# Head sums of a sliding-window attention by four accumulating DMAs, on one Trainium2 core

## The chip, the cores and the metric

The kernel runs on one core of a Trainium2 chip. The metric is the device time of one execution in microseconds (us). Before the change it is 1233.46 us (median of 3 runs, 1233.28 to 1234.1). A ratio of two kernels is the mean time of one kernel's runs over that of the other's of the same rounds, so it is not quite the ratio of the medians that are quoted.

Engines: PE is TensorE's matmul, PEld its weight load, DVE is VectorE, ACT is ScalarE, POOL is GpSimd, SP is SyncE.

## The reference

Two identical layers of attention and a dense GELU block, in bfloat16, over 2048 tokens of width 1024. Attention has 32 heads of 32 dimensions. Each token sees 8 keys: its own and those 2, 4, ..., 14 tokens back.

```python
def _A_ref(x, wqkv, wo):
    B, S, D = x.shape
    H = 32; Dh = D // H
    W, dil = 8, 2
    qkv = (x @ wqkv).reshape(B, S, 3, H, Dh).transpose(2, 0, 3, 1, 4)
    q, k, v = qkv[0], qkv[1], qkv[2]
    idx = jnp.arange(S)[:, None] - (jnp.arange(W) * dil)[None, :]
    mask = idx >= 0
    ...                                     # kg, vg: k and v at idx
    logits = jnp.einsum("bhsd,bhswd->bhsw", q, kg) * Dh ** -0.5
    logits = jnp.where(mask[None, None, :, :], logits, -1e9)
    o = jnp.einsum("bhsw,bhswd->bhsd", _softmax(logits, axis=-1), vg)
    return o.transpose(0, 2, 1, 3).reshape(B, S, D) @ wo

def _B_ref(x, w1, b1, w2, b2):              # F = 3584
    return _gelu(x @ w1 + b1) @ w2 + b2

x = x + _A_ref(_layernorm(x), wqkv, wo);  x = x + _B_ref(_layernorm(x), w1, b1, w2, b2)   # twice
```

## The kernel before

The work is cut into 8 groups: 2 layers of 4 token groups of 512 tokens each. Groups 0 to 3 are the first layer. A group of 512 tokens is four token tiles of 128 (`NTT = 4`). TensorE does the projections of all groups one after the other. VectorE computes the attention of one group while TensorE is busy with another.

The head dimension lies as follows. Head h's 32 dimensions are spread over 8 chunks c and over four partitions 4h + j. VectorE multiplies q and the eight shifted k's of a chunk into `prod[128, 4 tiles, 8 shifts, 128 tokens]` (the tile is called `big` in the profile, and there are only three such buffers), and adds the eight chunks together. What remains is the *head sum*: adding the four partitions j of each head. The kernel before had two ways to do this.

- For groups 0 and 1, TensorE multiplies by a matrix of ones and zeros, `smat`, 32 columns wide; the four token tiles go to four strips of partitions of one PSUM tile `L`.
- For groups 2 to 7, four DMAs copy the four token tiles into another large buffer `Lq`, and VectorE adds its four slices.

```python
def head_sum(n, last=True):                  # groups 0 and 1
    ...
    for wh in range(2):
        for tb in range(NTT):
            mm(L[tb * H:(tb + 1) * H, wh * 4:(wh + 1) * 4, :], lhsT=smat[:],
               rhs=prod[:, tb, wh * 4:(wh + 1) * 4, :], start=start,
               stop=last, skip_group_check=True, tile_position=(0, tb * H))

def gather(n):                               # groups 2 to 7
    s = st[n]
    prod = s["prods"].pop(0)
    Lq = bigp.tile([P, HP, W, P], BF16, name="big")
    for tb in range(NTT):
        pool.dma_start(Lq[tb * H:(tb + 1) * H, :, :, :], prod[:, tb, :, :])

def attend(n):
    e = smp.tile([P, W, P], F32, name="e")
    if "Lq" in s: ...                        # three adds of Lq's slices into e; L = e
    else:
        head_sum(n)
        L = s.pop("L")
    ...                                      # mask; mx = max over w; e = L - mx
    act.on = 1 < n < N - 1                   # exp in program order among ACT's other work
    act.activation(e[:], e[:], ACT.Exp, scale=SCALE)
    act.on = False
    ...                                      # z = 1 / sum over w; a = e * z

def spread(n):                               # weights to all partitions, by way of DRAM
    for tb in range(NTT):
        pool.dma_start(a_d[:, :, tb * P:(tb + 1) * P], a[tb * H:(tb + 1) * H, :, :])
    for j in range(HP):
        pool.dma_start(abc[j::HP, :, :], a_d[:, :, :])
```

`av(n, c)` then forms the weighted sums over v, chunk by chunk, into `oT` (8 chunks of about 4.3 us of VectorE), and `gen_wo(n)` multiplies `oT` by the output projection. `act.copy` and `act.activation` also empty TensorE's PSUM banks: q, k and v chunks are cast out, and the dense block's hidden values go through GELU into `hT`. PSUM is the memory, in banks, that TensorE's sums go to and that the other engines empty. TensorE fills one bank (8 matmuls of 512 columns) in 1.72 us: while it runs without a wait, ScalarE's casts start 1.72 to 1.73 us apart.

The schedule around the first two groups; `(u, f)` means that f is put in after step u of TensorE's generator, and `hold` pins VectorE's program order:

```python
stage(q1, sides=at(6, attend, 0) + at(6, spread, 0) + at(6, hold) + each(new_prod, 1, 8, 1, 0, 4) + each(av, 0, 12, 1))
q2 = gen_qkv(2, defer=True)
stage(q2, 18)
new_prod(1, 4)
...
stage(gen_wo(0))
...
stage(gen_ffn1(0), sides=at(5, attend, 1) + at(5, spread, 1) + at(5, hold) + each(new_prod, 2, 2, 1)
      + at(10, gather, 2) + at(10, hold) + each(av, 1, 10, 2, 0, 4))
...
for n in range(1, N - 2):
    ...
    gather(n + 2)
    stage(gen_ffn1(n), sides=(at(20, attend, n + 2) if n + 3 == N else []) + each(av, n + 1, 8, 2, 3, 8))
```

## Time and profile before

| | before |
|---|---|
| time, median | 1233.46 us |
| span of the profiled execution | 1231.1 us |
| TensorE busy | 1226.2 us |
| VectorE busy | 870.0 us |
| TensorE's waits that the profile lists | 1.1 and 0.7 us |

The page of the kernel before begins with busy time by engine. PEclk is the granted clock of TensorE, that is the share of its full speed at which the chip lets it run, in tenths in 40 equal slices of the span (9 is 90% or more). The last line is the chain of work that ended last, by engine.

```profile
span 1231.1 us, 13996 instructions
...
PE 1226.2 (100%) x5789; PEld 632.7 (51%) x5789; DVE 870.0 (71%) x892; ACT 307.1 (25%) x491; POOL 123.0 (10%) x230
...
PEclk9999999999999999999999999999999999999999
...
PE 99%; DVE 0%; DMA 0%; ACT 0%; issue 0%
```

The list of TensorE's waits before: what waited, for whom; total us, times, longest.

```profile
PE acc L118 <- DVE big L93: 1.1, 1, 1.1
PE L L213 <- ACT xnT L93: 0.7, 1, 0.7
```

Both waits lie in the start-up. So TensorE bounds the kernel and nothing else costs time now. But the margin is thin in two places. VectorE's timeline before, around the end of group 0's weighted sums (columns: start, busy us, instruction, count, and in brackets the idle time just before it with what ended it):

```profile
123.41 0.76 DVE L93 TENSOR_TENSOR oT<-big 128x512 bf16<-128x512 bf16 x2
124.08 2.29 DVE L93 TENSOR_TENSOR big<-qT,kT 128x4096 bf16<-128x4096 bf16 x1
...
247.00 0.76 DVE L93 TENSOR_TENSOR oT<-big 128x512 bf16<-128x512 bf16 x2
```

TensorE's timeline at the same places:

```profile
125.40 13.99 PE L118 MATMUL acc<-wt,oT 128*128 128x512 bf16 x64
...
246.94 13.98 PE L118 MATMUL acc<-wt,oT 128*128 128x512 bf16 x64
```

`oT` of group 0 is complete at 124.17, and TensorE starts on it at 125.40: 1.2 us to spare. `oT` of group 1 is complete at 247.76, after TensorE has started at 246.94; only because the last chunks are needed last does nothing wait.

### The profile page before, as it was taken

What the parts mean: (1) busy time and instruction counts of PE and PEld (TensorE: products, weight loads), DVE (VectorE), ACT (ScalarE), POOL (GpSimd) and SP (SyncE); (2) the same over time, 40 slices, a digit from 0 to 9 for tenths busy, and PEclk for the clock granted to TensorE, in tenths of its full rate; (3) what the DMA queues carried; (4) which work ended last, traced back from release to release, by engine and by line L of the source; (5) the groups of instructions that cost most, each with busy time, mean ns of one, the idle gap of its engine ahead of it and who ended that gap; (6) DMA issues with size and microseconds to landing.
All of it is one profiled execution on the core that took longest, in us unless ns stands there. A gap on an engine that the chain in (4) does not pass through costs nothing.

```text
span 1231.1 us, 13996 instructions
## 1 busy us (share of the span) xinstructions
PE 1226.2 (100%) x5789; PEld 632.7 (51%) x5789; DVE 870.0 (71%) x892; ACT 307.1 (25%) x491; POOL 123.0 (10%) x230
## 2 busy tenths in 40 slices
PE   9999999999999999999999999999999999999999
PEld 7666544456444564445544465444654444444444
DVE  8989899995996999376992779927599698012001
ACT  4343152014310143202431024310244101400310
POOL 3010011101021102200031000210000102000000
PEclk9999999999999999999999999999999999999999
DMA  9954677756487658756476565766666569546441
GB/s 301 289 179 142 177 220 183 210 140 230 147 197 226 177 165 180 220 170 186 149 187 222 172 171 169 174 222 196 171 183 157 186 200 198 166 158 196 153 136 53
DMA packets 219359, 226.63 MB, mean 184 GB/s; under 512 B 68562, under 2 KB 187488, under 8 KB 216224
## 3 DMA queue, kind: packets, MB, share of 16 engines
q1 hardware_dynamic: 214704, 208.69, 57.1%
q0 software_dynamic: 4592, 17.05, 5.7%
q8 instruction: 45, 0.74, 0.2%
q14 instruction: 18, 0.15, 0.0%
HBM read 197.40 MB, written 6.29 MB: 165 GB/s over the span
## 4 chain that ended last, share of the span: by engine, by line
PE 99%; DVE 0%; DMA 0%; ACT 0%; issue 0%
PE acc L118 99%; DMA x<-in_A_x_dram 0%; DVE stats L93 0%; PE acc L213 0%; PE L L118 0%; PE L L213 0%; ACT xnT L93 0%; DVE xn L93 0%; DVE x L93 0%; DVE mv L93 0%; PE acc L183 0%; DVE rstd L93 0%
## 5 line engine op out<-in xcount | busy, mean ns | idle before, releaser
L118 PE MATMUL acc<-xnT,wt 128*128 128x512 bf16 (+1 forms) x3392 | 720.8, 375 | 0.0
L118 PEld LDWEIGHTS <-wt 128*128 128x128 bf16 x3392 | 400.3, 119 | 318.8 <-issue 1.6
L118 PE MATMUL acc<-wt,hT 128*128 128x512 bf16 (+1 forms) x1820 | 388.1, 376 | 0.0
L118 PEld LDWEIGHTS <-hT 128*128 128x128 bf16 x1820 | 178.1, 98 | 209.0
L93 DVE TENSOR_TENSOR big<-big 128x2048 bf16<-128x2048 bf16 (+2 forms) x184 | 245.6, 1360 | 2.9
L93 ACT ACTIVATE hT<-acc,b1T 128x512 bf16<-128x512 f32 x224 | 152.5, 688 | 331.3 <-PE acc L118 331.2
L93 DVE TENSOR_TENSOR big<-qT,kT 128x4096 bf16<-128x4096 bf16 x64 | 143.8, 2286 | 26.7 <-ACT kT L93 26.1
L93 DVE TENSOR_TENSOR big<-abc,vT 128x4096 bf16<-128x4096 bf16 x64 | 144.8, 2287 | 24.3 <-DMA abc<-a_d 23.7
L93 DVE TENSOR_TENSOR tmp<-acc,b2bc 128x512 f32<-128x512 f32 x56 | 38.7, 690 | 148.4 <-PE acc L118 144.9
L93 ACT CAST qT<-acc 128x512 bf16<-128x512 f32 (+1 forms) x72 | 38.0, 542 | 341.4 <-PE acc L118 341.4
L118 PE MATMUL acc<-wt,oT 128*128 128x512 bf16 x448 | 97.9, 379 | 0.0
L93 DVE BATCH_NORM_STATS2 stats<-x 128x6 f32<-128x512 bf16 x128 | 83.5, 680 | 3.3 <-DMA x<-in_A_x_dram 2.6
L118 PEld LDWEIGHTS <-oT 128*128 128x128 bf16 x448 | 43.9, 98 | 52.8
L93 DVE TENSOR_TENSOR x<-acc,big 128x512 bf16<-128x512 f32 (+1 forms) x9 | 5.7, 633 | 90.0 <-PE acc L118 90.0
L93 POOL TENSOR_TENSOR rstd<-mv,eps_t 128x1 f32<-128x1 f32 x56 | 22.5, 402 | 434.4 <-DVE mv L93 434.3
L93 ACT CAST vT<-acc 128x512 bf16<-128x512 f32 x64 | 37.5, 586 | 83.1 <-PE acc L118 83.1
L93 ACT CAST kT<-acc 128x512 bf16<-128x512 f32 x64 | 37.3, 588 | 66.7 <-PE acc L118 66.6
L93 DVE TENSOR_TENSOR x<-acc,x 128x512 bf16<-128x512 f32 x64 | 42.6, 669 | 3.9 <-PE acc L118 3.8
L93 POOL TENSOR_TENSOR rstd<-rstd,mhalf 128x1 f32<-128x1 f32 x56 | 41.6, 743 | 4.4
L93 DVE TENSOR_SCALAR xn<-x,mv,rstd 128x1024 bf16<-128x1024 bf16 x52 | 28.4, 546 | 17.1 <-POOL rstd L93 16.9
L93 DVE TENSOR_TENSOR x<-tmp,x 128x512 bf16<-128x512 f32 x56 | 38.6, 690 | 1.6
L93 DVE TENSOR_REDUCE z<-e 128x128 f32<-128x1024 f32 x8 | 15.4, 1926 | 33.7 <-ACT e L93 33.7
(64 smaller groups left out, 252.0 us busy)
## 6 DMA issues: line engine op xcount, KB each, us to landing
wt<-in_B_w_dram SPq DMA_DIRECT2D x56, 1024.0 KB, 7.1
wt<-in_B_w_dram SPq DMA_DIRECT2D x64, 896.0 KB, 5.1
wt<-in_A_wqkv_dram SPq DMA_DIRECT2D x46, 1024.0 KB, 5.7
wt<-in_A_wo_dram SPq DMA_DIRECT2D x16, 1024.0 KB, 5.0
abc<-a_d POOLq DMA_DIRECT2D x32, 256.0 KB, 5.0
big<-big POOLq DMA_DIRECT2D x24, 256.0 KB, 7.0
x<-in_A_x_dram SPq DMA_DIRECT2D x16, 256.0 KB, 5.7
out_dram<-x SPq DMA_DIRECT2D x31, 128.0 KB, 2.4
```

The source lines that it names most:

```text
L93: inst = f(*args, **kwargs)
L118: return pe(nc.tensor.matmul(*args, **kwargs))
```

## The change

All groups now take one way. `e` is a float32 tile with partition 4h + tb, so that the four token tiles of a head lie side by side. Four DMAs add `prod`'s partitions j = 0, 1, 2, 3 of every head into it. That takes the matmuls, the copy into a large buffer and VectorE's three adds away. The attention weights go back to all partitions by four DMAs within SBUF, the memory in which the engines' tiles lie, without the trip through DRAM. The maximum and the sum over the window become folds by halves instead of a strided reduce. The two PSUM banks of `L` go to the accumulators (8 instead of 6). In the start-up, the second late transpose stands two chunks later, and six casts of q move behind the loop.

```diff
     def gather(n):
         s = st[n]
         prod = s["prods"].pop(0)
-        Lq = bigp.tile([P, HP, W, P], BF16, name="big")
-        s["Lq"] = Lq
-        for tb in range(NTT):
-            pool.dma_start(Lq[tb * H:(tb + 1) * H, :, :, :], prod[:, tb, :, :])
+        e = smp.tile([P, W, P], F32, name="e")
+        s["e"] = e
+        for j in range(HP):
+            if j == 0:
+                pool.dma_start(e[:], prod[j::HP, :, :, :])
+            else:
+                pool.dma_start(e[:], prod[j::HP, :, :, :], accum_op=ALU.add)
+
+    def fold(e, op):
+        t = iop.tile([P, W // 2, P], F32, name="tmp")
+        vec.tensor_tensor(out=t[:], in0=e[:, 0:4, :], in1=e[:, 4:8, :], op=op)
+        vec.tensor_tensor(out=t[:, 0:2, :], in0=t[:, 0:2, :], in1=t[:, 2:4, :], op=op)
+        vec.tensor_tensor(out=t[:, 0, :], in0=t[:, 0, :], in1=t[:, 1, :], op=op)
+        return t[:, 0, :]
 
     def attend(n):
-        ...                                  # head_sum, or three adds of Lq's slices
-        vec.tensor_reduce(out=mx[:], in_=L[:].rearrange("p w t -> p t w"), axis=AX.X, op=ALU.max)
+        e = s.pop("e")
+        mx = fold(e, ALU.max)
...
     def spread(n):
-        abc = attp.tile([P, W, T], BF16, name="abc")
-        a_d = dram.tile([H, W, T], BF16, name="a_d")
-        for tb in range(NTT):
-            pool.dma_start(a_d[:, :, tb * P:(tb + 1) * P], a[tb * H:(tb + 1) * H, :, :])
+        abc = attp.tile([P, NTT, W, P], BF16, name="abc")
         for j in range(HP):
-            pool.dma_start(abc[j::HP, :, :], a_d[:, :, :])
+            pool.dma_start(abc[j::HP, :, :, :], a[:])
...
-                if (kq, c) in ((2, 5), (3, 1)):
+                if (kq, c) in ((2, 5), (3, 3)):
                     transpose_on_pe(*first_late.pop(0))
...
-        stage(q1, sides=at(6, attend, 0) + at(6, spread, 0) + at(6, hold) + each(new_prod, 1, 8, 1, 0, 4) + each(av, 0, 12, 1))
+        stage(q1, sides=at(0, gather, 0) + each(new_prod, 1, 8, 1, 0, 3) + at(10, hold) + at(10, attend, 0) + at(10, spread, 0)
+              + at(11, new_prod, 1, 3) + at(11, hold) + each(av, 0, 12, 1))
...
         stage(q2, sides=each(new_prod, 1, 0, 1, 5, 8))
+        gather(1)
...
-    stage(gen_ffn1(0), sides=at(5, attend, 1) + at(5, spread, 1) + at(5, hold) + each(new_prod, 2, 2, 1)
+    stage(gen_ffn1(0), sides=each(new_prod, 2, 2, 1, 0, 4) + at(6, hold) + at(6, attend, 1) + at(6, spread, 1) + at(6, hold) + each(new_prod, 2, 6, 1, 4, 8)
           + at(10, gather, 2) + at(10, hold) + each(av, 1, 10, 2, 0, 4))
```

The four DMAs of a gather follow one another. All four go to the same `e`, and in the trace GpSimd waits for `e<-big` before each of the later three issues (2.62, 8.37 and 3.33 us in group 0).

## The prediction

> **What bounds it now.** TensorE. The page gives PE busy 1226.2 of 1231.1 us, the chain that ended last is 99% PE, and the list of waits shows PE waiting twice (1.1 and 0.7 us, in the start-up). VectorE (870.0 us, 71%) costs nothing unless its results reach a matmul late.

> **Where that is close.** VectorE's timeline has only two gaps of 2 us between 28.7 and 126 us. It finishes oT of group 0 at 124.2; PE starts on oT at 125.4. From 143.3 to 247.8 it is busy throughout: oT of group 1 is complete at 247.8, PE starts on it at 246.9 and needs the last chunks about 1.3 us later. So slack is about 2.7 us at the first output projection and 0.5 us at the second. From the third on it is over 30 us, at the last about 8 us.

> **Removed.** 16 head-sum matmuls (2 x 0.55 us on the chain); six times three float32 adds (1.2 us each) on VectorE, off the critical path; two reduces of 1.92 us per group, replaced by folds of about 1.2 us (estimate from 1.2 us per 1024 float32 columns); one of two DMA hops of the spread (2 to 4 us). The PSUM shuffle may save 0.7 us at the start.

> **Added.** For groups 0 and 1 too, four DMAs that wait for each other: each adds 256 KB of bfloat16 into 512 KB of float32. The trace's 64 KB DMAs from GpSimd land 2.6 us after issue [...]. Packets of that queue took about 0.24 us for 3.7 KB (5.7% of 16 engines' span, 4592 packets); 128 packets of 4 KB on 16 engines make 2 us more, the accumulation perhaps that again. Estimate: 4 to 6.5 us each, about 20 us a gather.

> **On the critical path.** The instruction order shows that the third new product (group 0) or fourth (group 1) after a gather starts waits for all four DMAs, since the gather still reads one of three large buffers. So VectorE has 4.6 us of work under gather 0 and 9.2 us under gather 1.
> - Gather 0 starts at 62.8 and lands at 83; then 14 us (one product, three adds, mask, fold, subtract), exp and rest 5, spread 6.5 with nothing beside it, weighted sums 34.2: oT complete at about 142 to 143. PE stalls about 17 us.
> - Gather 1: VectorE idle 11 us; with savings and slack PE stalls 9 to 10 us at the second output projection.
> - Later gathers: hidden behind four weighted sums (17 us) and slack.
> Lost PE time is not regained: 1233.5 - 2 + 17 + 9 is about 1257 us. Each us of one gather DMA counts about 8 us in total, so the range is wide.

> **Predicted: 1257 us, 8 in 10 between 1243 and 1278.** Faster by over 2%: 0.02; within 2%: 0.52; slower by over 2%: 0.46.

> **Right or wrong by:** PE shows two waits on VectorE's weighted sums, about 17 us near 125 us and 10 us near 265 us, nothing else above 2 us; VectorE idles about 15 us before the third product of group 1 and 11 before the fourth of group 2, both ended by the gather's DMAs, and 6 us for the spread of group 0. Issue to landing of a gather DMA: 4 to 6.5 us. VectorE busy falls by some 30 us without effect.

> **What would make it wrong.** Accumulating DMAs much faster (3 us: near 1241) or slower (8 us: near 1285, with ScalarE, whose exp stands among its PSUM evictions, stalling PE as well). GpSimd waits inside each gather, so a layer norm's rstd behind one could come late. Weight loads could slow the gathers.

From the numbers, an estimate is 2.6 + 2 us, and 2 more if accumulation costs that again: 4.6 to 6.6 us a DMA, where the author recorded 4 to 6.5 and about 20 us a gather. That accumulation might cost the packets' time again was the author's guess; measured later, it is 2.15 us of packets against 1.40 with no weight load in flight. 1233.5 - 2 + 17 + 9 is 1257.5, about 1257.

## The result, and the profile after

The changed kernel is correct and takes 1282.66 us (median of 6 runs, 1281.64 to 1284.61). The kernel before took 1233.39 us in the same rounds (6 runs, 1232.98 to 1234.1). The ratio is 1.040, with a 95% interval of 1.0386 to 1.0413: slower by 4%, about 49 us. It was predicted slower by 24 us, with 1278 as the upper end of the range.

The same lines of the page, after:

```profile
span 1280.9 us, 13955 instructions
...
PE 1237.6 (97%) x5773; PEld 635.1 (50%) x5773; DVE 837.2 (65%) x906; ACT 305.5 (24%) x491; POOL 96.2 (8%) x205
...
PEclk9998799999999999999999999999999899999999
...
PE 77%; DVE 10%; DMA 3%; issue 2%; ACT 1%; POOL 0%; DVEq 0%; POOLq 0%; ACTq 0%
```

Two things happened to TensorE at once. Its busy time rose by 11.4 us although it has 16 matmuls fewer, and the time in which it is not busy rose from 4.9 to 43.3 us, by 38.4. Together that is the 49.8 us by which the span grew. The clock line tells why the busy time rose: it is no longer all nines, and the mean granted clock of this run is 0.981.

The list of TensorE's waits after:

```profile
PE acc L117 <- DVE oT L92: 21.5, 4, 7.8
PE acc L117 <- ACT hT L92: 10.5, 2, 5.3
PE acc L117 <- ACT vT L92: 6.8, 1, 6.8
...
```

Where they are, from TensorE's timeline after:

```profile
104.93 27.66 PE L117 MATMUL acc<-xnT,wt 128*128 128x512 bf16 x120 [6.84 <-ACT vT L92]
...
139.22 1.03 PE L117 MATMUL acc<-wt,oT 128*128 128x512 bf16 x2 [5.77 <-DVE oT L92]
147.77 15.04 PE L117 MATMUL acc<-wt,oT 128*128 128x512 bf16 x58 [7.52 <-DVE oT L92]
...
221.67 8.29 PE L117 MATMUL acc<-xnT,wt 128*128 128x512 bf16 x24 [5.33 <-ACT hT L92]
...
279.53 0.72 PE L117 MATMUL acc<-wt,oT 128*128 128x512 bf16 x2 [0.37 <-DVE oT L92]
288.09 14.86 PE L117 MATMUL acc<-wt,oT 128*128 128x512 bf16 x58 [7.83 <-DVE oT L92]
...
1000.50 7.99 PE L117 MATMUL acc<-xnT,wt 128*128 128x512 bf16 x24 [5.16 <-ACT hT L92]
```

Call these five places A (105), B (139 and 148), C (222), D (280 and 288) and E (1000). Their idle time sums to 38.8 us. B and D are the two output projections that had 1.2 us and nothing to spare before; there `oT` comes late. At A, C and E it is not VectorE that holds TensorE up directly but ScalarE, which doesn't empty the PSUM banks.

All of it goes back to the gather. GpSimd's timeline after shows group 0's four DMA issues, each with the wait before it:

```profile
62.78 0.55 POOL L92 DMA_DIRECT2D e<-big  x1 [34.15 <-DVE big L92]
65.95 0.93 POOL L92 DMA_DIRECT2D e<-big  x1 [2.62 <-DMA e<-big]
75.25 0.90 POOL L92 DMA_DIRECT2D e<-big  x1 [8.37 <-DMA e<-big]
79.48 0.88 POOL L92 DMA_DIRECT2D e<-big  x1 [3.33 <-DMA e<-big]
```

VectorE's timeline after shows what the gather holds up, in group 0, group 1 and group 7:

```profile
89.62 2.29 DVE L92 TENSOR_TENSOR big<-qT,kT 128x4096 bf16<-128x4096 bf16 x1 [17.46 <-DMA e<-big]
...
113.75 4.49 DVE L92 TENSOR_TENSOR big<-abc,vT 128x4096 bf16<-128x4096 bf16 x2 [5.59 <-DMA abc<-a]
...
208.94 2.29 DVE L92 TENSOR_TENSOR big<-qT,kT 128x4096 bf16<-128x4096 bf16 x1 [17.53 <-DMA e<-big]
...
989.38 2.29 DVE L92 TENSOR_TENSOR big<-abc,vT 128x4096 bf16<-128x4096 bf16 x1 [11.29 <-DMA e<-big]
```

The third new product after gather 0 starts, and the fourth after gather 1, need the large buffer that the gather still reads. VectorE stands idle for 17.5 us each time. From the first issue to the moment when VectorE may go on, gather 0 takes 26.8 us (62.78 to 89.6), gather 1 26.1 (182.84 to 208.9).

ScalarE's timeline after, at A, shows how the late gather reaches TensorE by another way:

```profile
84.32 0.59 ACT L92 CAST vT<-acc 128x512 bf16<-128x512 f32 x1 [1.14 <-PE acc L117]
84.93 1.28 ACT L92 ACT_TABLE_LOAD   x1
103.35 1.06 ACT L92 ACTIVATE e<-e 128x1024 f32<-128x1024 f32 x1 [17.14 <-DVE e L92]
104.32 2.52 ACT L92 CAST vT<-acc 128x512 bf16<-128x512 f32 x5
```

The exponential of group 0 stands in ScalarE's instruction stream between two casts of v. It waits 17.14 us for VectorE's subtraction, and the casts behind it wait with it. TensorE has 8 PSUM banks in this kernel, and fills one in 1.72 us, so it can go on for 13.8 us without ScalarE. From the start of the cast at 84.32 that is until 98.1, which is just when TensorE stops. The bank is free again at 104.9: 6.8 us lost. The same sum gives 5.1 us for E (last GELU at 981.57, next at 999.76, plus 0.7, less 13.8), where the profile shows 5.16, and 5.3 for C (202.57 to 220.93), where it shows 5.33. So an exponential that waits among evictions is free up to a limit, and then costs TensorE the whole excess.

The clock is the second loss. The trace's clock record has five pieces at half speed. This table puts them beside the idle times:

| place | TensorE idle before | half clock (us from the span's start) | length | TensorE busy in it |
|---|---|---|---|---|
| A | 6.84 | 101.37 to 108.20 | 6.83 | 3.27 |
| B | 5.77, 7.52 | 135.50 to 152.57 | 17.07 | 5.83 |
| C | 5.33 | 220.84 to 227.66 | 6.83 | 5.99 |
| D | 7.83 | 282.28 to 292.52 | 10.24 | 4.43 |
| E | 5.16 | 999.07 to 1005.90 | 6.83 | 5.40 |

### The profile page after: what moved, and what is told of

The parts are those of the page before. It is cut to its first block, busy times and chain, and to the rows that moved or that the text cites. A ratio compares the mean times of both kernels' runs of the same rounds, so it can differ in the third digit from the quotient of the medians.

```text
span 1280.9 us, 13955 instructions
## 1 busy us (share of the span) xinstructions
PE 1237.6 (97%) x5773; PEld 635.1 (50%) x5773; DVE 837.2 (65%) x906; ACT 305.5 (24%) x491; POOL 96.2 (8%) x205
## 4 chain that ended last, share of the span: by engine, by line
PE 77%; DVE 10%; DMA 3%; issue 2%; ACT 1%; POOL 0%; DVEq 0%; POOLq 0%; ACTq 0%
PE acc L117 77%; DVE big L92 8%; DMA e<-big 3%; DVE tmp L92 1%; DVE oT L92 0%; DVE stats L92 0%; DVE e L92 0%; POOL e L92 0%; ACT e L92 0%; DMA abc<-a 0%; ACT L92 0%; DVE x L92 0%; ACT hT L92 0%; POOL abc L92 0%; DVE xn L92 0%
## 5 line engine op out<-in xcount | busy, mean ns | idle before, releaser
L92 DVE TENSOR_TENSOR big<-big 128x1024 bf16<-128x1024 bf16 (+2 forms) x184 | 244.4, 1360 | 1.7
L92 DVE TENSOR_TENSOR big<-qT,kT 128x4096 bf16<-128x4096 bf16 x64 | 144.0, 2286 | 74.0 <-ACT kT L92 38.4
L117 PE MATMUL acc<-wt,oT 128*128 128x512 bf16 x448 | 103.6, 392 | 21.5 <-DVE oT L92 21.5
L92 POOL DMA_DIRECT2D e<-big x32 | 26.2, 818 | 439.0 <-ACT hT L92 203.9
L92 POOL TENSOR_TENSOR rstd<-mv,eps_t 128x1 f32<-128x1 f32 x56 | 14.9, 265 | 434.0 <-DVE mv L92 434.0
L92 DVE TENSOR_SCALAR xn<-x,mv,rstd 128x1024 bf16<-128x1024 bf16 x52 | 28.1, 546 | 21.3 <-POOL rstd L92 16.7
L92 POOL TENSOR_TENSOR rstd<-rstd,mhalf 128x1 f32<-128x1 f32 x56 | 31.7, 565 | 4.4
```

The costliest lines, as they stand in the source:

```text
L92: inst = f(*args, **kwargs)
L117: return pe(nc.tensor.matmul(*args, **kwargs))
```

## The experiments

The theory when these were planned: the late gathers cause all five places, directly (B, D) or by way of ScalarE (A, C, E), and each wait brings a stretch of half clock with it. A gather is long because four DMAs wait for each other and some of them wait behind weight loads. The rivals were a cost of accumulation itself, a cost of the new layout, folds or spread, and a clock loss that does not come from idleness. The experiments ran in other rounds than the changed kernel. The kernel before ran in all of these rounds (medians 1233.39, 1233.25 and 1233.49 us), so their times are set against 1282.66 us directly.

The trace's DMA packet records let one take a gather apart. For each DMA: the issue on GpSimd; the delay from the end of the issue to its first packet; the time from the first to the last packet; then 0.6 to 0.7 us until the next issue begins. This table shows group 0 in three kernels, the last two being experiments below:

| gather 0 | delays of the four DMAs | packets of the four DMAs | issues, sum | first issue to VectorE going on |
|---|---|---|---|---|
| after | 0.57, 4.49, 0.57, 3.99 | 1.40, 3.20, 2.15, 4.70 | 3.26 | 26.8 |
| without weight loads | 0.57, 0.57, 0.57, 0.56 | 1.40, 2.16, 2.15, 2.17 | 3.26 | 15.7 |
| plain DMAs | 0.57, 3.53, 0.57, 0.56 | 1.40, 2.61, 1.40, 1.39 | 2.19 | 16.7 |

In the longest of these delays (4.49 us) 657 pieces of 2 KB started on the weight queue; in the delays of 0.57 us of the same gather none did.

### 1. Head sums of groups 0 and 1 by matmul again

The rest of the change stays: the new layout and spread for all groups, accumulating gathers for groups 2 to 7. The sums of token tile tb now go to the partitions 4h + tb, spread over all 128, so this run uses a `smat` 128 columns wide.

```diff
-    smat = const.tile([P, H], BF16, name="smat")
+    smat = const.tile([P, P + NTT], BF16, name="smat")     # ones at column NTT-1+4h for partitions 4h..4h+3
...
-                mm(L[tb * H:(tb + 1) * H, wh * 4:(wh + 1) * 4, :], lhsT=smat[:],
-                   rhs=prod[:, tb, wh * 4:(wh + 1) * 4, :], start=start,
-                   stop=last, skip_group_check=True, tile_position=(0, tb * H))
+                mm(L[:, wh * 4:(wh + 1) * 4, :], lhsT=smat[:, NTT - 1 - tb:NTT - 1 - tb + P],
+                   rhs=prod[:, tb, wh * 4:(wh + 1) * 4, :], start=tb == 0, stop=tb == NTT - 1)
...
+        if n > 1:
+            L = e = s.pop("e")               # gathered, as in the changed kernel
         else:
             head_sum(n)
             L = s.pop("L")
```

The old schedule of groups 0 and 1 and the 6 + 2 PSUM banks of before go with it.

> Groups 0 and 1 take their head sums from matmuls again (16 full ones, so about 2 x 1.2 us more TensorE than before); everything else of the change stays: accumulating gathers for groups 2 to 7, the new spread, layout and folds. Theory (the latency of the gathers of groups 0 and 1 is the loss, group 7 a small part through the exp on ScalarE): 1233.4 + 2.4 + 5.2 (wait of group 7) + 2.7 (half clock after it) = about 1244 us, no TensorE wait on oT. Rival (spread, layout, folds or the larger PSUM ring cost as well): above 1255 us, with waits on oT left near 125 or 265 us.

Measured: correct, 1244.15 us (1239.51 to 1245.23, 4 runs), ratio 1.0082 (1.0065 to 1.0098). The list of TensorE's waits of this run:

```profile
PE acc L117 <- ACT hT L92: 6.6, 1, 6.6
PE acc L117 <- DVE big L92: 1.1, 1, 1.1
...
```

No wait for `oT` is left. So A to D come from the gathers of groups 0 and 1 and the schedule that goes with them; this run takes both away at once. The new spread and layout, which this kernel keeps, cause no wait, nor do the folds, which it keeps except for the maximum of groups 0 and 1. The one wait left is E (here at 958.65), in group 7. One of the four executions took 1239.51 us at a granted clock of 0.999, the others 1243.26 to 1245.23 at 0.996 or 0.997. Its trace was not kept; a shorter wait at E would fit, but that is not shown.

### 2. Group 7's softmax later among the GELUs

```diff
-        act.on = 1 < n < N - 1
+        act.on = 1 < n
...
-        stage(gen_ffn1(n), sides=(at(20, attend, n + 2) if n + 3 == N else []) + each(av, n + 1, 8, 2, 3, 8))
+        stage(gen_ffn1(n), sides=(at(25, attend, n + 2) if n + 3 == N else []) + each(av, n + 1, 8, 2, 3, 8))
```

`act.on = 1 < n` puts group 7's exponential into ScalarE's program order, and with `at(25, ...)` it comes five steps later there.

> The exp of group 7 comes five ffn1 units later in ScalarE's order, nothing else changes. Theory (TensorE waits 5.2 us near 1000 us only because ScalarE holds the evictions behind that exp, and then runs 5.3 us at half clock, 2.7 us lost): 1282.7 - 7.8 = about 1275 us and no wait in that stage. Rival (the wait comes from DMA contention or VectorE, not from the place of the exp): 1282 us, the wait only moves.

Measured: correct, 1274.62 us (1273.39 to 1275.74, 4 runs), ratio 1.0336 (1.0322 to 1.035), 8.0 us less than the changed kernel. TensorE's timeline of this run around place E:

```profile
949.63 51.32 PE L117 MATMUL acc<-xnT,wt 128*128 128x512 bf16 x237
1000.78 9.44 PE L117 MATMUL acc<-wt,hT 128*128 128x512 bf16 x43
```

TensorE works through. The 8.0 us are the wait of 5.16 and 2.7 of half clock (half of 5.40), which sum to 7.9. So a gather of the same length (27.7 us from first issue to last landing in both kernels) is free with its exponential further back. E takes both, though, the long gather and that place in ScalarE's order: in experiment 5, where gather 7 lands after 19.1 us, E is gone with the exponential in its old place.

### 3. Filler matmuls in TensorE's waits

Matmuls whose result nobody reads fill the three long waits for `oT`, so that TensorE is still late but not idle.

```diff
+    def filler(count):
+        if count:
+            ps = acc_tile()
+            for _ in range(count):
+                mm(ps[:], lhsT=ident[:], rhs=ident[:].unsqueeze(1).to_broadcast([P, NTT, P]), start=True, stop=True)
...
+                    if tt == dh == 0:
+                        filler({(0, 4): 24, (0, 6): 32, (1, 6): 32}.get((n, c), 0))   # by group n and chunk c of gen_wo
```

> Useless matmuls (24 and 32 before chunks 4 and 6 of the first output projection, 32 before chunk 6 of the second; about 5.2, 6.9 and 6.9 us at full clock) fill waits that TensorE has anyway; no wait is made shorter. Theory (the lower granted clock is caused by the idle stretch before it and costs half of the busy time under it: 5.75 and 4.34 us): about 1282.7 - 5.0 = 1277.7 us, granted clock 1.0 near 140 to 152 and 282 to 292 us. Rival (the clock falls for another reason, or the loss is not the clock): 1282.7 us or more.

Measured: correct, 1275.95 us (1275.57 to 1277.46, 5 runs), ratio 1.0349 (1.0335 to 1.0363), 6.7 us less than the changed kernel by medians, with 88 matmuls more. TensorE's timeline of this run at B:

```profile
134.19 5.34 PE L117 MATMUL acc<-ident 128*128 128x512 bf16 x24
139.85 0.72 PE L117 MATMUL acc<-wt,oT 128*128 128x512 bf16 x2 [0.31 <-DVE oT L92]
140.41 7.07 PE L117 MATMUL acc<-ident 128*128 128x512 bf16 x32
148.40 12.81 PE L117 MATMUL acc<-wt,oT 128*128 128x512 bf16 x58 [0.92 <-DVE oT L92]
```

The last 58 matmuls of the projection start as late as in the changed kernel (148.40 against 147.77), yet take 12.81 us instead of 15.04 there. At D it is 12.81 instead of 14.86. So the half clock follows from idleness. About 4.3 us of the gain are thus read off directly; of the profiled runs (1277.18 against 1282.72 us) the gain is 5.5. In the rest there is some luck: group 7's wait was 3.8 us in the profiled run and not 5.2, as its gather took 26.3 us to land and not 27.7. The half-clock pieces at A, C and E, where nothing was filled, are still there.

### 4. No weight loads beside gather 0 (wrong result)

The k and v projections of groups 1 and 2 use the q weights that are already there, so that four loads of 1 MB a group fall away. The result is wrong (relative error 1.10).

```diff
-        wk = load_qkv(1)
+        wk = wq if n in (1, 2) else load_qkv(1)
...
-            wv = load_qkv(2)
+            wv = wq if n in (1, 2) else load_qkv(2)
```

> Wrong result on purpose: groups 1 and 2 use their q weights for k and v too, so about 8 MB of weight loads near gather 0 are gone. Theory (a gather DMA waits behind weight loads in flight: 4.4 and 3.9 us in two of the four): each accumulating DMA of gather 0 takes about 4.3 us, the gather 16 to 17 us instead of 26.8; TensorE waits about 10 us less before the first output projection; about 1271 us. Rival (an accumulating DMA is slow by itself): gather 0 still takes 25 us or more, time above 1280 us.

Measured: 1271.66 us (1271.14 to 1272.42, 4 runs), ratio 1.0312 (1.0298 to 1.0327). GpSimd's timeline of this run:

```profile
63.62 0.54 POOL L92 DMA_DIRECT2D e<-big  x1 [34.16 <-DVE big L92]
66.78 0.93 POOL L92 DMA_DIRECT2D e<-big  x1 [2.62 <-DMA e<-big]
71.07 0.90 POOL L92 DMA_DIRECT2D e<-big  x1 [3.36 <-DMA e<-big]
75.30 0.89 POOL L92 DMA_DIRECT2D e<-big  x1 [3.33 <-DMA e<-big]
```

The wait of 8.37 us has become 3.36, and the last DMA lands 3.9 us after its issue instead of 10.0: each accumulating DMA now takes the same 4.2 to 4.3 us. Gather 0 takes 15.7 us instead of 26.8. The other seven gathers of this run still took 24.1 to 27.8 us to land. Of the 11 us saved, 7.4 are delays and 3.6 packets. Its gain of 11.0 us is in the main the vanished wait A with its half clock (6.84 + 1.6) and 2.1 us of waiting for `oT` (19.4 us in all, 21.5 in the changed kernel). It does not gain the whole 11 us at B: TensorE, not being stopped at A, now arrives at B earlier too.

### 5. A chain of plain DMAs (wrong result)

The four DMAs still follow each other, but the last three overwrite `e` instead of adding to it (relative error 0.88).

```diff
-                pool.dma_start(e[:], prod[j::HP, :, :, :], accum_op=ALU.add)
+                pool.dma_start(e[:], prod[j::HP, :, :, :])
```

> The changed kernel with the four gather DMAs still on one tile, one after the other, but without accumulation: each overwrites the sum (a wrong result on purpose, only the last head slice survives). Theory (a gather is long because four DMAs wait for each other and two of them wait behind weight loads in flight; accumulation itself adds about 0.35 us of issue and 0.75 us of packets to each of three DMAs): gather 0 shrinks from 26.8 us by only 3 to 6 us, to 21 to 24; the two output projections wait for the weighted sums about 3 to 5 us less each; 1270 to 1276 us against 1282.7. Rival (the accumulation is what makes the DMAs slow): each plain DMA lands about 3 us after its issue, the gather takes about 13 us, most waits go, and the time is 1245 to 1255 us.

Measured: 1263.79 us (1261.57 to 1265.06, 4 runs), ratio 1.0244 (1.023 to 1.0258). **This missed both expectations**: it lies between them. The list of TensorE's waits of this run:

```profile
PE acc L117 <- DVE oT L92: 23.4, 4, 7.8
PE acc L117 <- ACT hT L92: 3.3, 1, 3.3
...
```

Gather 0 shrank by 10 us, not by 3 to 6. From the table above: issues gave 1.1 us, packets 4.65, delays 4.4. What the theory had wrong is the packets. I had costed accumulation from the DMA that met no weight load (2.15 us instead of 1.40), but those that do meet one take 3.20 and 4.70 against 2.61 and 1.39 plain. Gather 1 shrank by only 2 us, since its delays grew by 1.0. To keep chance out of it, here are means over all eight gathers of a run, in us, with the landing of the last DMA as the end:

| | issues | delays | packets | first issue to landing |
|---|---|---|---|---|
| accumulating (after) | 3.3 | 9.3 | 11.2 | 26.2 |
| plain chain (this run) | 2.2 | 7.1 | 7.8 | 19.7 |

So accumulation costs about 4.5 us a gather directly (issues and packets). A further 2 us of delay vanished with it; whether that is accumulation or only other moments of issue, these runs do not tell apart. The rival (accumulation is all of it, 13 us a gather without it) falls as well: 7.1 us of delays remain, where four DMAs with nothing in flight have 2.3 (4 x 0.57).

The waits tell the rest. A and E are gone, C is down from 5.33 to 3.3, but the sum of the waits for `oT` *rose*, from 21.5 to 23.4. Again TensorE arrives earlier at the projections because nothing stopped it before. A wait that disappears early hands part of its time to the next.

### 6. Both repairs together

Experiment 1 with the two lines of experiment 2.

> The run with head sums by matmul for groups 0 and 1 (1244.2 us), and group 7's softmax five steps later in program order as in the run that moved it. The theory says that these two places, with the half clock that each wait brings, are all of the loss but the 2.4 us by which the wide head-sum matmuls are slower: the wait of 6.6 us near 958 us and about 2 to 3 us of half clock go, time 1235 to 1237.5 us, TensorE with no wait over 2 us and a granted clock of 1.00. Rival (the longer life of the float32 sum, the new spread or the folds cost something elsewhere as well): it stays above 1240 us.

Measured: correct, 1234.94 us (1234.76 to 1235.3, 4 runs), at the lower edge of what was expected, against 1233.49 for the kernel before in the same rounds; ratio 1.0012 (0.9998 to 1.0026). The page's clock line and the list of waits of this run:

```profile
PEclk9999999999999999999999999999999999999999
```

```profile
PE acc L217 <- DVE xn L92: 1.4, 1, 1.4
PE acc L117 <- DVE big L92: 1.1, 1, 1.1
PE L L217 <- ACT xnT L92: 0.7, 1, 0.7
```

The whole loss is gone within the noise, with 24 of the 32 accumulating DMAs still in place. Whether the remaining 1.4 us are real, the interval leaves open. One cost is seen in the groups of the profile, the head-sum matmuls, first before and then in this run (columns: busy us, mean ns of one, idle before):

```profile
L118 PE MATMUL L<-big,smat 128*32 128x512 bf16 x16 | 1.2, 384 | 0.0
```

```profile
L117 PE MATMUL L<-big,smat 128*128 128x512 bf16 x16 | 3.8, 379 | 0.0
```

The same 16 matmuls cost 3.8 instead of 1.2 us, 3.2 times as much by busy time. In the trace before, the four of one `wh`, one for each strip of 32 columns, start within 0.01 us and the next four 0.22 us later, so four run beside each other, and 8 take 0.61 us; with 128 columns 8 take 1.89 us in this run. So the wider rows of the new layout are not free on the tensor engine.

### 7. One detail of the start-up alone

The kernel before, with the second late transpose two chunks later, as the change has it.

```diff
-                if (kq, c) in ((2, 5), (3, 1)):
+                if (kq, c) in ((2, 5), (3, 3)):
```

> The kernel before, with one detail of the change alone: the second late transpose of the start-up stands two chunks later. Theory: the wait of 0.66 us of TensorE at 14.5 us goes and nothing else changes: 1232.7 to 1233.1 us against 1233.4, a gain of 0.3 to 0.7 us, the same by the 2% verdict. Rival (the start-up gain of the changed kernel comes from the two extra PSUM banks, not from the order): no change, 1233.2 to 1233.6 us.

Measured: correct, 1232.95 us (1232.59 to 1233.36, 5 runs) against 1233.49 (1232.88 to 1234.41, 9 runs); ratio 0.9996 (0.9982 to 1.0009). The median falls within the theory's range, but the interval holds 1, and the profiled run's wait only shrank from 0.7 to 0.2 us while another of 0.3 us for a weight load came up. A gain is not shown. So no version that beats the kernel before was found. With TensorE busy 1226.2 of 1231.1 us there is little left to find in this direction.

## Why the prediction was wrong

The prediction had the mechanism of two of the five places, and about half of the size. Three of its steps failed: the length of a gather (about 20 us, measured 26.2 to its landing), the path through ScalarE ("nothing else above 2 us", measured A, C and E), and the half clock, which it did not count (12.5 us).

| term of the sum | predicted | measured | |
|---|---|---|---|
| head-sum matmuls and start-up saved | -2 | -1.6 | 1.2 matmuls, 0.4 less idle time outside A to E |
| stalls from gather 0 | 17 | 20.1 | A 6.84 and B 13.29 |
| stalls from gather 1 | 9 | 13.5 | C 5.33 and D 8.20 |
| later gathers | 0 | 5.2 | E |
| half clock | not in it | 12.5 | all five places |
| sum | 24 | 49.7 | the span grew by 49.8 |

- **"The page gives PE busy 1226.2 of 1231.1 us ... So slack is about 2.7 us at the first output projection and 0.5 us at the second": right.** B and D are at the two projections that it named, ended by the weighted sums.
- **"the third new product (group 0) or fourth (group 1) after a gather starts waits for all four DMAs": right.** VectorE's timeline shows exactly these two instructions waiting on `e<-big`. The waits are 17.5 us, predicted 15 and 11. The spread was predicted at 6 us of VectorE idle and showed 5.59. VectorE's busy time fell by 33 us, as said, without effect.
- **"Estimate: 4 to 6.5 us each, about 20 us a gather": this step failed.** The median from issue to landing, 6.0 us, is inside the range. The total is not: gathers took 26 to 27.7 us to land, except one of 24. Gather 0 let VectorE go on at 89.6 and not at 83, and `oT` was complete at 148.1 and not at 142 to 143, so this length is about the whole error on that path. Where no weight load ran beside it, a gather took 15.7 us, so the estimate's pieces were not too low. What was missing is the delay beside weight loads in flight (experiment 4 shows that they cause it in gather 0): the delays are 9.3 us a gather on average, and 2.3 where nothing is in flight. The prediction named it only in its last sentence and gave it no number. The 26.2 us of an average gather can thus be read as a sum (of 26.4): 12.7 for four plain DMAs in a quiet chain (4 x (0.55 + 0.57 + 1.40 + 0.65), an estimate from the pieces above), 4.5 for accumulation, 7.0 for longer delays and 2.2 for plain packets that are slower beside weight loads (7.8 less 4 x 1.40).
- **Half clock: left out, and the largest single error.** The prediction counted the idle time of two stalls that it put at 17 and 9 to 10 us and added no half clock to them. The trace before could not have shown it: its two waits are 1.1 and 0.7 us, and its granted clock is 1.000. 12.5 us of 49.7 are this. Experiment 3 shows it by keeping TensorE busy.
- **"nothing else above 2 us" and "Later gathers: hidden": failed for ScalarE.** A, C and E are waits for evictions that stand behind an exponential. The prediction mentions this only for DMAs of 8 us. The threshold was computable: 13.8 us of PSUM against the time that the exponential waits. For group 7 it was tight even before: from one GELU to the next it was 942.98 to 952.55, 10.3 us with the 0.7 of the second, and 6 banks are 10.3 us. That the later gathers were hidden from the *projections* was right, and experiment 2 shows that for group 7 another place of the exponential is enough.

What stays open: by which rule weight loads delay GpSimd's DMAs. Experiment 4 shows that they cause the delays of gather 0 (4.49 and 3.99 us with them, 0.57 and 0.56 without); for the other gathers it is taken over from gather 0. That A and C would go with the exponential further back, as E did, was not tried.

## What to carry to other kernels

When a change puts a longer latency on the way to a bound engine, count the slack at every consumer, and that means also the engine that empties PSUM: an instruction that waits in its stream is free only for as many banks as TensorE can still fill (8 x 1.72 us here, which met three of the five places to within 0.1 us). Add to a long stall of TensorE the half clock that followed it here (from 3.67 us on, and not yet at 3.34); it made a third more of 38.8 us. Cost a chain of dependent DMAs with the traffic that runs beside it, not from quiet ones: the same gather took 15.7 us alone and 26.8 us beside weight loads.
